# The first attention block reordered (keys hashed ahead of queries, the projection split on GpSimd, the second head turned inside unit zero's scores), and the token-buffer fills issued two units later

## Chip, cores and metric

The kernel runs on 1 core of one Trainium2 chip. The metric is the device time of one execution in microseconds (us), taken as the median of several runs. Before the change it is 513.87 us, the median of 3 runs from 513.18 to 513.99.

## What is computed

Three stages follow one another: attention masked by a hash of queries and keys (LSH), a mixture of experts with one expert per token, and a SoLU layer with a norm.

```python
q_bits = (np.einsum('bhsd,dk->bhsk', q, proj) > 0).astype(np.int64)
k_bits = (np.einsum('bhsd,dk->bhsk', k, proj) > 0).astype(np.int64)
q_bucket = np.sum(q_bits * 2 ** np.arange(n_bits), axis=-1)        # n_bits = 6, k the same
mask = q_bucket[:, :, :, None] == k_bucket[:, :, None, :]
scores = np.where(mask, scale * np.matmul(q, k.transpose(0, 1, 3, 2)), -1e9)
attn = np.exp(scores - np.max(scores, axis=-1, keepdims=True))
out = np.matmul(attn / (np.sum(attn, axis=-1, keepdims=True) + 1e-09), v)
...
h = np.maximum(x[mask] @ w1[e], 0.0); out[mask] = gate_w * eom * (h @ w2[e])   # per expert e
...
h = x @ w_in; solu = h * softmax(h); out = layer_norm(solu) * g_ln @ w_out
```

Shapes: q, k and v are [2, 8, 768, 64], proj is [64, 6], there are 8 experts and 1536 tokens of width 512.

## The kernel before

The 16 (batch, head) pairs are taken two heads at a time: eight blocks n = 0 to 7. A block has 12 units (two halves of the queries, three tiles of 128 queries, two heads), 96 units in all. `emit_s` (L592) writes a unit's scores with four TensorE matmuls: two multiply q (high and low halves in 16 bits) with k, two add the hash mask by multiplying the query's bit rows (tile `cm`, called "c") with the key's bit rows and low halves (tile "b"). `emit_max` (L602 to L606) takes the row maximum on VectorE, `emit_exp` (L617) the exponential on ScalarE, `steps_t` (L629, L631) transposes the result of the unit two before between the score matmuls, and `emit_pv` (L653) multiplies with v. A hand-written schedule orders everything: `at(i, f, slot)` hangs a background step on unit i, and `due` emits it there; each engine runs its instructions in the order in which the code emits them.

The hash bits need operands with the head dimension on the partitions. For blocks 1 to 7 GpSimd splits q and k (`split`, L367 to L382) and the DMA queue of SP turns them (`trans`, L394 to L406: q, then k, then the low halves b). Block 0 can't wait for that: `first` (L412 to L526) splits on VectorE, ScalarE and GpSimd and turns on TensorE (`pe`, L420), head 0 first. `q_hi`, `q_lo`, `k_hi` and `k_lo` are the splits; `bits_mm` (L542 to L548) multiplies with the split projection `pw`, and `bits_rows` (L554) compares the result with thresholds and writes the bit rows. `setup` (L215) splits the projection `pj` into `pw`: 15 small operations on VectorE and three copies on GpSimd. Head 1 of block 0 follows, turned before the first score matmul: its q and k transposes stand in front of unit 0's scores on TensorE.

Two more pieces matter. `setup_late`, hung on unit 2, loads the gate weights into `rg` and g_ln into `g1` with five small DMAs on SP's queue, behind a GpSimd memset of `rg`. `zero(e)`, hung on unit 8 + 4e, fills expert e's rows of the token buffer `xs` in DRAM with zeros from a tile that GpSimd clears once.

In `first`, the order in which head 0 is handled is this:

```python
q_t(0, pq); k_hi(0); k_t(0, pk)
act.copy(out=d["q", 0], in_=pq)
q_hi(1, True); k_lo(0); setup(); l_t(0, pl)
act.copy(out=d["k", 0], in_=pk)
...
bits_mm(0, "q", (0, 1), mq)
bits_mm(0, "k", (0, 1), mk)
```

Of the kernel before, what the change touches and what calls it, by code (L numbers as in the profile page):

```python
# [21 lines left out]
def kernel(  # L22
# [15 lines left out]
    nc = tc.nc  # L38
# [175 lines left out]
    def setup():  # L214

        NB2 = 2 * NBIT
        sc = early.tile([128, 512], I32, tag="db", name="db", bufs=2)[0:64]
        pi = sc[:, 0:NB2]
        pf = sc.bitcast(F32)[:, NB2:4 * NB2].rearrange("p (a b) -> p a b", a=3)
        p16 = sc.bitcast(F16)[:, 8 * NB2:13 * NB2].rearrange("p (a b) -> p a b", a=5)  # L220
        d = nc.vector
# [4 lines left out]
        d.tensor_copy(out=p16[:, 3], in_=pf[:, 0])  # L226
        d.tensor_scalar(out=pf[:, 1], in0=pi, scalar1=0.125, scalar2=None, op0=ALU.mult)
        d.tensor_tensor(out=p16[:, 4], in0=pf[:, 0], in1=p16[:, 3], op=ALU.subtract)
        d.tensor_tensor(out=pf[:, 2], in0=pf[:, 0], in1=pf[:, 1], op=ALU.subtract)
        d.tensor_copy(out=p16[:, 0], in_=pf[:, 1])  # L230
        d.tensor_copy(out=p16[:, 1], in_=pf[:, 2])
        o = slice(0, NB2)
        a, b = slice(0, 64), slice(64, 128)
        d.tensor_copy(out=pw[b, 1:3, o], in_=p16[:, 3:5])
        d.tensor_tensor(out=p16[:, 2], in0=pf[:, 2], in1=p16[:, 1], op=ALU.subtract)
        d.tensor_copy(out=pw[a, 8, o], in_=p16[:, 3])
        d.tensor_copy(out=pw[a, 7, o], in_=p16[:, 1])
        d.tensor_copy(out=pw[a, 0:3, o], in_=p16[:, 0:3])
        d.tensor_copy(out=pw[b, 7, o], in_=p16[:, 2])
# [20 lines left out]
    def setup_late():  # L260
        ie = const.tile([128, E], I32, name="ie")
        it = const.tile([128, B, NS], I32, name="it")
        g = nc.gpsimd
        g.memset(rg, 0.0)
# [6 lines left out]
        nc.sync.dma_start(out=g1, in_=g_ln.rearrange("(f p) -> p f", p=128))  # L271
        g.iota(ie, pattern=[[1, E]], base=0, channel_multiplier=0)
# [39 lines left out]
    def attention(es):  # L312
# [96 lines left out]
        def first():  # L409
# [21 lines left out]
            def q_hi(h, on_act):  # L431
                if on_act:
                    act.activation(out=tq[:, h, :, h], in_=q_[:, h], func=AF.Copy, scale=QK_S)
                else:
                    dve.tensor_scalar(out=tq[:, h, :, h], in0=q_[:, h], scalar1=QK_S, scalar2=None, op0=ALU.mult)

            def q_lo(h):
                dve.scalar_tensor_tensor(out=tq[:, h, :, 1 - h], in0=q_[:, h], scalar=QK_S, in1=tq[:, h, :, h],
                                         op0=ALU.mult, op1=ALU.subtract)
# [27 lines left out]
            def lo_pool(o, i, hi):  # L467
                nc.gpsimd.tensor_scalar(out=i, in0=i, scalar1=QK_S, scalar2=1.0, op0=ALU.mult, op1=ALU.mult)
                nc.gpsimd.tensor_tensor(out=o, in0=i, in1=hi, op=ALU.subtract)

# [4 lines left out]
            nc.gpsimd.memset(cm.bitcast(F32)[96:128, :, 0], 0.0)  # L475
            nc.gpsimd.memset(cm.bitcast(F32)[32:64, :, 1], 0.0)
            q_hi(0, False)
            q_lo(0)
# [12 lines left out]
            mq, mk = t32(ps_m, "m"), ps_s.tile([128, 2, 512], F32, tag="s", name="s")[:, 0]  # L491
# [6 lines left out]
            lo_pool(tq[:, 1, :, 0], q_[:, 1], tq[:, 1, :, 1])  # L498
            k_hi(1)
            lo_pool(tl[:, :, 1], k_[:, 1], tk[:, 1, :, 0])  # L500
            begin(1)
            pq1, pk1 = t16(ps_v, "v"), t16(ps_t, "t0")
            q_t(1, pq1)
            k_t(1, pk1)
            act.copy(out=d["q", 1], in_=pq1)
            act.copy(out=d["k", 1], in_=pk1)
            nc.gpsimd.tensor_copy(out=d["c", 1][row(1)], in_=d["q", 1][row(1)])
            mid = {}

            def later1():  # L510
                pl1 = t16(ps_v, "v")
                l_t(1, pl1)
                act.copy(out=d["b", 1][row(1)], in_=pl1[row(1)])
                bits_rows(0, "q", 1, mq)

            def later2():
                mid["q"], mk1 = t32(ps_m, "m"), t32(ps_v, "v")
                bits_mm(0, "q", (2, 3), mid["q"])
                bits_mm(0, "k", (2, 3), mk1)
                bits_rows(0, "q", 2, mid["q"])  # L520
                bits_rows(0, "k", 2, mk1)
                bits_rows(0, "k", 3, mk1)

            at(0, later1, slot=0)
            at(1, later2, slot=1)
            at(3, lambda: bits_rows(0, "q", 3, mid["q"]))  # L526
# [4 lines left out]
        def bits_mm(n, which, groups, m):  # L531

            d = op[n]
            for i in range(3):
                for g in groups:
# [5 lines left out]
                    if which == "q":  # L541
                        nc.tensor.matmul(o, pw[:, 3 * h + i], flat(d["q", h])[:, cs], tile_position=(0, 32 * g), **k_)  # L542
                    elif i < 2:
                        nc.tensor.matmul(o, pw[:, 7 * i], flat(d["k", h])[:, cs], tile_position=(0, 32 * g), **k_)
                    elif n == 0:
                        nc.tensor.matmul(o, pw[r, 8 + h], flat(d["b", h])[r, cs], tile_position=(64 * h, 32 * g), **k_)
                    else:
                        nc.tensor.matmul(o, pw[:, 8 + h], flat(d["b", h])[:, cs], tile_position=(0, 32 * g), **k_)  # L548

# [459 lines left out]
        for e in range(E):  # L1009
            at(8 + 4 * e, zero, e)  # L1010
# [22 lines left out]
    with tc.manual_schedule():  # L1033
        with ExitStack() as es:
# [14 lines left out]
            for i in range(NU):  # L1049
                a_("emit_s")(i, a_("steps_t")(i - 2) if 2 <= i else iter(()))  # L1050
# [457 lines left out]
```

## Time and profile before

| what | value |
|---|---|
| median of 3 runs | 513.87 us |
| profiled execution, its own time | 513.23 us |
| its span, first to last instruction | 511.5 us |
| TensorE busy | 496.9 us (97% of the span) |
| VectorE busy | 388.2 us (76%) |
| ScalarE busy | 320.9 us (63%) |
| GpSimd busy | 281.9 us (55%) |
| granted TensorE clock, mean | 0.999 |

Busy times count instructions between their recorded start and end. PE is TensorE's matmul side, PEld its weight loads, DVE is VectorE, ACT ScalarE, POOL GpSimd, SPq the DMA queue of SyncE. Attention takes the span up to about 235 us, the experts run to about 375 us, the last layer to the end.

### The profile page before, as it was taken

Reading aid. Unit: us, or ns where it says so; the run is one execution under the profiler, and the core shown is the slowest. Engines: PE = TensorE matmul, PEld = TensorE weight load, DVE = VectorE, ACT = ScalarE, POOL = GpSimd, SP = SyncE. Lnnn points to the kernel's source line nnn. Section 1 sums busy time; section 2 is a strip of 40 time slices with the busy share of each in tenths; the row PEclk is TensorE's granted clock in tenths of the full one; section 3 lists DMA queues with packets and bytes.
Section 4 is the critical chain, followed back from the end, with each engine's and each line's share of the span. In section 5 each row is a group of like instructions: output and inputs, shape, how many; then the busy total and the mean of one; then the engine's idle time right before and its main releaser. Section 6 shows DMA issues by size and latency. Waiting matters only on the chain. (4 is left out here: it accounts for less than half of the span.)

```text
span 511.5 us, 12503 instructions
## 1 busy us (share of the span) xinstructions
PE 496.9 (97%) x4716; PEld 385.1 (75%) x4716; DVE 388.2 (76%) x922; ACT 320.9 (63%) x601; POOL 281.9 (55%) x438
## 2 busy tenths in 40 slices
PE   7899999999999999999999999999999999999994
PEld 5678787888888887887999999999984444444443
DVE  7787888888889888877779799979935987656610
ACT  6778787887887788886256566556623445534421
POOL 6999897869879898644366587322012113221131
PEclk9999999999999999999999999999999999999999
DMA  7398969772946675500499999998800246442281
GB/s 263 57 214 185 245 162 232 195 204 78 187 142 108 187 202 121 161 1 22 157 305 278 318 309 271 268 324 277 279 12 0 42 82 97 108 106 62 62 145 41
DMA packets 107182, 83.21 MB, mean 163 GB/s; under 512 B 80624, under 2 KB 89456, under 8 KB 107120
## 3 DMA queue, kind: packets, MB, share of 16 engines
q1 hardware_dynamic: 104816, 76.09, 59.1%
q0 software_dynamic: 2304, 6.31, 3.2%
q8 instruction: 37, 0.61, 0.5%
q14 instruction: 25, 0.20, 0.1%
HBM read 51.43 MB, written 9.97 MB: 120 GB/s over the span
## 5 line engine op out<-in xcount | busy, mean ns | idle before, releaser
L629 PE MATMUL t<-ident,p 128*128 128x128 f32 x576 | 126.1, 275 | 0.6
L617 ACT ACTIVATE p<-s,mx 128x768 f32<-128x768 f32 x96 | 95.8, 998 | 36.4 <-DVE mx L606 22.5
L602 DVE TENSOR_REDUCE mx<-s 128x1 f32<-128x768 f32 x96 | 91.5, 953 | 28.4 <-PE s L592 22.4
L631 ACT COPY pt<-t 128x384 f32<-128x384 f32 x192 | 85.6, 480 | 7.4 <-PE t L629 6.2
L629 PEld LDWEIGHTS t<-ident,p 128*128 128x128 f32 x576 | 77.8, 141 | 15.6 <-ACT pt L631 9.0
L653 PE MATMUL v<-pt,v 128*64 128x128 f32 x1128 | 72.0, 277 | 0.0
L653 PEld LDWEIGHTS v<-pt,v 128*64 128x64 f32 x1128 | 60.6, 137 | 7.7 <-issue 6.8
L1446 PE MATMUL o<-wo,zT 128*128 128x512 f16 (+1 forms) x312 | 63.7, 363 | 0.1
L1246 PE MATMUL a<-hh,wb 128*128 128x224 f16 (+5 forms) x256 | 63.4, 251 | 0.1
L131 POOL TENSOR_SCALAR dm<-dm 128x512 f32<-128x512 f32 x16 | 33.0, 2061 | 55.5 <-ACT dm L126 55.3
L1374 PE MATMUL h<-wi,yT 128*128 128x512 f16 x288 | 63.5, 379 | 0.0
L1247 PE MATMUL a<-hh,wb 128*128 128x224 f16 (+5 forms) x256 | 63.4, 251 | 0.0
L1248 PE MATMUL a<-hh,wb 128*128 128x224 f16 (+5 forms) x256 | 63.4, 251 | 0.0
L592 PE MATMUL s<-k,q 128*128 128x384 f16 x192 | 59.0, 329 | 1.2 <-ACT p L617 1.2
L592 PE MATMUL s<-b,cm 128*128 128x384 f16 x192 | 57.2, 326 | 0.9 <-DVE b L554 0.9
L1219 PE MATMUL a<-xw,wa 128*128 128x224 f16 (+5 forms) x224 | 55.1, 249 | 0.0
L1218 PE MATMUL a<-xw,wa 128*128 128x224 f16 (+5 forms) x224 | 55.1, 249 | 0.0
L1217 PE MATMUL a<-xw,wa 128*128 128x224 f16 (+5 forms) x224 | 55.1, 249 | 0.0
L1446 PEld LDWEIGHTS <-zT 128*128 128x128 f16 x312 | 30.5, 98 | 32.2 <-issue 0.4
L1374 PEld LDWEIGHTS <-yT 128*128 128x128 f16 x288 | 28.2, 98 | 33.7
L1452 POOL DMA_INDIRECT out_dram<-o,tok x12 | 12.6, 1048 | 53.3 <-issue 42.4
L168 ACT ACTIVATE wb<-raw 128x1024 f16<-128x1024 f32 x24 | 25.3, 1055 | 22.1 <-DMA raw<-in_moe_w_dram 22.0
(275 smaller groups left out, 1017.7 us busy)
## 6 DMA issues: line engine op xcount, KB each, us to landing
raw<-in_moe_w_dram SPq DMA_DIRECT2D x64, 512.0 KB, 6.1
raww<-in_moe_w_in_dram SPq DMA_DIRECT2D x8, 512.0 KB, 5.1
raww<-in_moe_w_out_dram SPq DMA_DIRECT2D x8, 512.0 KB, 6.4
xs<-raw SPq DMA_DIRECT2D x8, 448.0 KB, 4.4
v<-in_v_dram SPq DMA_DIRECT2D x8, 384.0 KB, 6.7
q<-in_q_dram SPq DMA_DIRECT2D x6, 384.0 KB, 4.3
k<-in_k_dram SPq DMA_DIRECT2D x6, 384.0 KB, 6.5
cm<-q SPq DMA_DIRECT2D x14, 96.0 KB, 2.1
```

Source lines behind the costliest of these rows:

```text
L592: nc.tensor.matmul(t[:, c, 0:SB], d[x, h][:, s], flat(d[y, h])[:, c * SB:(c + 1) * SB], start=first, stop=not first)
L602: nc.vector.tensor_reduce(out=mx[:, 0:1], in_=t[:, :, 0:SB], op=ALU.max, axis=AX.XY)
L617: nc.scalar.activation(out=p, in_=s_t.pop(i)[:, :, 0:SB], func=AF.Exp, scale=mx[:, 1:2], bias=mx[:, 2:3], accum_out=sums[j][:, qt, h:h + 1])
L629: nc.tensor.transpose(t[:, g * 128:(g + 1) * 128], p[:, c, g * 128:(g + 1) * 128], ident)
L631: nc.scalar.copy(out=pt[i][:, 3 * c:3 * c + 3], in_=t[:, 0:SB].rearrange("p (g c) -> p g c", g=3))
L653: nc.tensor.matmul(o[64 * h:64 * h + 64], vt[:, h, c], ph[h][:, c], start=(c == 0), stop=(c == NS - 1), tile_position=(0, 64 * h))
L1217: nc.tensor.matmul(ps[:, i, 0:n], w[:, 0, kk, fs], xw[:, 0, kk], start=(kk == 0), stop=False)
L1246: nc.tensor.matmul(ps, w[:, 0, f, ds], hh[:, 0, f], start=(f == 0), stop=False)
L1247: nc.tensor.matmul(ps, w[:, 0, f, ds], hh[:, 1, f], start=False, stop=False)
L1248: nc.tensor.matmul(ps, w[:, 1, f, ds], hh[:, 0, f], start=False, stop=(f == KF - 1))
L1374: nc.tensor.matmul(ps[:, c], yT[:, a, kk, ts], w_i[:, w, kk, c * 512:(c + 1) * 512], start=(kk == 0 and a == 0 and w == 0), stop=(kk == KD ...
L1446: nc.tensor.matmul(ps, zT[:, KF * a + f], w_o[:, w, f, cs], start=(f == 0 and a == 0 and w == 0), stop=(f == KF - 1 and a == 1))
```

## The change

Four parts. (1) `pj` is loaded from ScalarE's DMA queue before anything else there, not from SP's between the second q and the second k. (2) `setup` is cut into four pieces; GpSimd does the nine steps that lead to the rounded projection and one copy into `pw`, VectorE two steps and four copies, and GpSimd's other three copies come after head 1's split. (3) In `first`, q of head 0 is split by VectorE and ScalarE in halves, k is copied out and hashed before q, both halves of the key bits are compared in one operation (`bits_k2`, at one tile position in two banks), head 1's low half of k moves from GpSimd to VectorE, and head 1's q and k are turned between unit 0's q-k and mask matmuls. The query bits of units 6 onward (`bits_rows` with groups 1 and 3) move to units 3 and 4. (4) The five gate and g_ln loads move from unit 2 to unit 0, their memset to the start; two memsets of `cm`, used by block 1, move from the start to unit 1; the fills of the token buffer move from unit 8 + 4e to unit 10 + 4e.

```diff
@@ setup
-        d.tensor_copy(out=pf[:, 0, 0:NBIT], in_=pj)
-        d.tensor_scalar(out=pf[:, 0, NBIT:], in0=pj, scalar1=-1.0, scalar2=None, op0=ALU.mult)
-        d.tensor_scalar(out=pi, in0=pf[:, 0], scalar1=8.0, scalar2=None, op0=ALU.mult)
...
-        nc.gpsimd.tensor_copy(out=pw[b, 9, o], in_=p16[:, 3])
-        nc.gpsimd.tensor_copy(out=pw[b, 3:6, o], in_=p16[:, 0:3])
-        nc.gpsimd.tensor_copy(out=pw[a, 4:6, o], in_=p16[:, 3:5])
+        def gpsimd():
+            g.tensor_copy(out=pf[:, 0, 0:NBIT], in_=pj)
+            g.tensor_scalar(out=pf[:, 0, NBIT:], in0=pj, scalar1=-1.0, scalar2=1.0, op0=ALU.mult, op1=ALU.mult)
+            g.tensor_scalar(out=pi, in0=pf[:, 0], scalar1=8.0, scalar2=1.0, op0=ALU.mult, op1=ALU.mult)
+            g.tensor_scalar(out=pf[:, 1], in0=pi, scalar1=0.125, scalar2=1.0, op0=ALU.mult, op1=ALU.mult)
+            g.tensor_tensor(out=pf[:, 2], in0=pf[:, 0], in1=pf[:, 1], op=ALU.subtract)
+            g.tensor_copy(out=p16[:, 0], in_=pf[:, 1])
+            g.tensor_copy(out=p16[:, 1], in_=pf[:, 2])
+            g.tensor_tensor(out=p16[:, 2], in0=pf[:, 2], in1=p16[:, 1], op=ALU.subtract)
+            g.tensor_copy(out=pw[a, 0:3, o], in_=p16[:, 0:3])
...
+        def vector_late():
+            d.tensor_copy(out=pw[b, 1:3, o], in_=p16[:, 3:5])
+            d.tensor_copy(out=pw[a, 8, o], in_=p16[:, 3])
+            d.tensor_copy(out=pw[a, 7, o], in_=p16[:, 1])
+            d.tensor_copy(out=pw[b, 7, o], in_=p16[:, 2])
@@ first
-            q_hi(0, False)
-            q_lo(0)
+            pool, pool_late, vec, vec_late = setup()
+            q_hi(0, False, half[0])
+            q_hi(0, True, half[1])
+            for a in half:
+                q_lo(0, a)
+            pool()
+            vec()
             pq, pk, pl = t16(ps_t, "t0"), t16(ps_t, "t1"), t16(ps_v, "v")
             q_t(0, pq)
             k_hi(0)
             k_t(0, pk)
+            act.copy(out=d["k", 0], in_=pk)
+            k_lo(0)
+            vec_late()
+            l_t(0, pl)
             act.copy(out=d["q", 0], in_=pq)
-            q_hi(1, True)
-            k_lo(0)
-            setup()
-            l_t(0, pl)
-            act.copy(out=d["k", 0], in_=pk)
+            dve.tensor_copy(out=d["b", 0][row(0)], in_=pl[row(0)])
             dve.tensor_copy(out=d["c", 0][row(0)], in_=d["q", 0][row(0)])
-            dve.tensor_copy(out=d["b", 0][row(0)], in_=pl[row(0)])
...
+            bits_k2(0, 0, mk)
             bits_mm(0, "q", (0, 1), mq)
-            bits_mm(0, "k", (0, 1), mk)
+            r = slice(64, 96)
+            nc.vector.tensor_scalar(out=flat(d["b", 0])[r].rearrange("p (b x) -> p b x", b=2), in0=mk[0:32, :, 0:SB],
+                                    scalar1=thr[r, 1:2], scalar2=-MASK, op0=ALU.is_le, op1=ALU.mult)
             bits_rows(0, "q", 0, mq)
-            bits_rows(0, "k", 0, mk)
-            bits_rows(0, "k", 1, mk)
...
+            def second():
+                yield
+                k_t(1, pk1)
+                act.copy(out=d["k", 1], in_=pk1)
+                q_t(1, pq1)
+                act.copy(out=d["q", 1], in_=pq1)
+                yield
...
-            at(3, lambda: bits_rows(0, "q", 3, mid["q"]))
+            at(3, lambda: bits_rows(0, "q", 1, mq))
+            at(4, lambda: bits_rows(0, "q", 3, mq))
+            return second()
@@ bits_k2 (new)
+            for i in range(3):
+                for c in range(2):
+                    cs = slice(c * SB, (c + 1) * SB)
+                    o = m[0:32, c, 0:SB]
...
+                        nc.tensor.matmul(o, pw[:, 7 * i], flat(op[n]["k", h])[:, cs], tile_position=(0, 0), **k_)
@@ the rest
-            at(8 + 4 * e, zero, e)
+            at(10 + 4 * e, zero, e)
+        nc.scalar.dma_start(out=pj, in_=proj)
-                if h == 1 and nm == "q":
-                    nc.sync.dma_start(out=pj, in_=proj)
-            A["first"]()
+            nc.gpsimd.memset(rg, 0.0)
+            second = A["first"]()
             A["load"](1)
+            A["at"](0, gate_load)
             A["at"](2, setup_late)
-                a_("emit_s")(i, a_("steps_t")(i - 2) if 2 <= i else iter(()))
+                a_("emit_s")(i, a_("steps_t")(i - 2) if 2 <= i else iter(()) if i else second)
```

`gate_load` is the part of `setup_late` that issued the five DMAs.

How the instructions move, first on TensorE, from the hash of head 0 to unit 0's mask matmuls (`tp` is a transpose in PSUM, `tb` and `s` hold hash sums, `s` also the scores, `qs` and `ks` are split q and k). Before:

```order
L542 MATMUL tb<-q_197,pw 32x384
...
L544 MATMUL s<-k_198,pw 32x384
...
L546 MATMUL s<-b_199,pw 32x384
...
L420 MATMUL tp<-ident_72,qs 128x128
...
L420 MATMUL tp<-ident_72,ks 128x128
...
L592 MATMUL s<-k_198,q_197 128x384
...
L592 MATMUL s<-b_199,cm 128x384
```

and now:

```order
L582 MATMUL s<-k_199,pw 32x384
...
L584 MATMUL s<-b_200,pw 32x384
...
L565 MATMUL tb<-q_198,pw 32x384
...
L628 MATMUL s<-k_199,q_198 128x384
...
L430 MATMUL tp<-ident_72,ks 128x128
...
L430 MATMUL tp<-ident_72,qs 128x128
...
L628 MATMUL s<-b_200,cm 128x384
```

The keys' hash now stands ahead of the queries', and head 1's transposes stand between unit 0's q-k and mask matmuls, k ahead of q.

On ScalarE, from its first instruction to head 1's copies. Before:

```order
L1027 ACT_TABLE_LOAD
L1027 ACTIVATE warm<-warm 128x1
L442 ACTIVATE ks<-k 128x768
L483 COPY q_197<-tp 128x768
L433 ACTIVATE qs<-q 128x6x64
L488 COPY k_198<-tp 128x768
L442 ACTIVATE ks<-k 128x768
L505 COPY q_274<-tp 128x768
L506 COPY k_275<-tp 128x768
```

and now:

```order
L1056 DMA pj<-in_proj_dram 64x6
L1062 ACT_TABLE_LOAD
L1062 ACTIVATE warm<-warm 128x1
L445 ACTIVATE qs<-q 128x3x64
L454 ACTIVATE ks<-k 128x768
L496 COPY k_199<-tp 128x768
L500 COPY q_198<-tp 128x768
L512 CAST qs<-q 128x6x64
L454 ACTIVATE ks<-k 128x768
L524 COPY k_272<-tp 128x768
L526 COPY q_271<-tp 128x768
```

The copy of k comes before that of q, and head 1's q split no longer stands between the two.

On SP's queue, from the last weight load of the start to block 1's transposes. Before:

```order
L182 DMA raw<-in_moe_w_dram 128x1024
L394 DMA_TRANSPOSE q_371<-qs 128x6x128
L394 DMA_TRANSPOSE q_373<-qs 128x6x128
L400 DMA cm<-q_371 64x768
L400 DMA cm<-q_373 64x768
L269 DMA rg<-in_moe_w_gate_dram 64x4x8
L269 DMA rg<-in_moe_w_output_gate_dram 64x4x8
L269 DMA rg<-in_moe_w_gate_dram 64x4x8
L269 DMA rg<-in_moe_w_output_gate_dram 64x4x8
L271 DMA g_93<-in_moe_g_ln_dram 128x8x1
L394 DMA_TRANSPOSE k_467<-ks 128x6x128
```

and now:

```order
L182 DMA raw<-in_moe_w_dram 128x1024
L274 DMA rg<-in_moe_w_gate_dram 64x4x8
L274 DMA rg<-in_moe_w_output_gate_dram 64x4x8
L274 DMA rg<-in_moe_w_gate_dram 64x4x8
L274 DMA rg<-in_moe_w_output_gate_dram 64x4x8
L276 DMA g_93<-in_moe_g_ln_dram 128x8x1
L404 DMA_TRANSPOSE q_377<-qs 128x6x128
L404 DMA_TRANSPOSE q_379<-qs 128x6x128
L410 DMA cm<-q_377 64x768
L410 DMA cm<-q_379 64x768
L404 DMA_TRANSPOSE k_467<-ks 128x6x128
```

The five small loads no longer stand between block 1's q and k transposes.

## Rows read from the trace of the kernel before

**Rows 1.** Stretches: from:to, length, busy (count) of PE, PEld, DVE, ACT, POOL, clock, DMA.

```profile
4.52:9.84 5.32, 3.70 (x45) 2.63 (x45) 5.04 (x22) 3.15 (x6) 2.97 (x7) 1.00 0.98 305
...
12.00:18.00 6.00, 3.94 (x31) 2.62 (x25) 5.31 (x12) 4.13 (x9) 5.75 (x10) 1.00 0.36 77
18.00:20.00 2.00, 1.93 (x11) 1.09 (x10) 1.18 (x3) 2.00 (x6) 2.00 (x5) 1.00 0.74 145
...
32.00:230.00 198.00, 197.72 (x2163) 161.69 (x2163) 164.96 (x409) 159.48 (x343) 162.61 (x252) 1.00 0.66 165
...
250.00:502.00 252.00, 251.72 (x2068) 185.94 (x2066) 184.15 (x364) 126.64 (x188) 81.30 (x84) 1.00 0.65 172
```

**Rows 2.** Timeline, first block: start us, us, engine, line, operation [idle before <-releaser].

```profile
0.73 1.28 ACT L1027 ACT_TABLE_LOAD   x1 [0.73 <-PEq L1492]
...
3.18 0.69 DVE L435 TENSOR_SCALAR qs<-q 128x384 f16<-128x384 f32 x1 [0.72 <-DMA q<-in_q_dram]
3.71 0.84 ACT L442 ACTIVATE ks<-k 128x768 f16<-128x768 f32 x1 [1.48 <-DMA k<-in_k_dram]
4.98 0.50 PE L420 MATMUL tp<-ident,ks 128*128 128x128 f16 x6
5.88 0.53 ACT L433 ACTIVATE qs<-q 128x384 f16<-128x384 f32 x1
6.30 0.79 ACT L488 COPY k<-tp 128x768 f16<-128x768 f16 x1
...
7.45 0.50 PE L544 MATMUL s<-k,pw 128*32 128x384 f16 x4
7.87 0.91 POOL L469 TENSOR_TENSOR qs<-q,qs 128x384 f16<-128x384 f32 x1
7.90 0.61 DVE L554 TENSOR_SCALAR cm<-tb,thr 32x384 f16<-32x384 f32 x1
7.92 0.34 PE L546 MATMUL s<-b,pw 64*32 64x384 f16 x2
8.43 1.24 DVE L554 TENSOR_SCALAR b<-s,thr 32x384 f16<-32x384 f32 x2
9.52 0.49 PE L592 MATMUL s<-k,q 128*128 128x384 f16 x2
9.84 0.49 PE L592 MATMUL s<-b,cm 128*128 128x384 f16 x2
```

**Rows 3.** Timeline of TensorE at block 1's key bits: hash, then unit 9's scores.

```profile
30.54 0.51 PE L544 MATMUL m<-k,pw 128*32 128x384 f16 x8
...
31.68 0.34 PE L548 MATMUL m<-b,pw 128*32 128x384 f16 x2 [0.26 <-DMA b<-kl]
31.95 0.34 PE L592 MATMUL s<-k,q 128*128 128x384 f16 x1
```

**Rows 4.** Timeline of TensorE at the same place of block 2.

```profile
59.26 0.51 PE L544 MATMUL m<-k,pw 128*32 128x384 f16 x8
...
59.86 0.34 PE L592 MATMUL s<-k,q 128*128 128x384 f16 x1
```

**Rows 5.** Timeline of SP's DMA queue, the gate loads and block 1's transposes.

```profile
20.59 0.68 SPq L269 DMA_DIRECT2D rg<-in_moe_w_gate_dram  x1
...
23.96 2.60 SPq L394 DMA_TRANSPOSE k<-ks  x2
26.61 3.54 SPq L406 DMA_TRANSPOSE b<-kl  x2
```

**Rows 6.** Landing of `pj` (view of that tile).

```profile
DMA to landing us min/median/max: 3.0/3.0/3.0
```

**Rows 7.** Timeline of two small GpSimd operations in a row.

```profile
21.84 0.20 POOL L280 TENSOR_SCALAR iota_s<-iota 128x8 f32<-128x8 f32 x1
22.11 0.20 POOL L281 TENSOR_SCALAR ord<-iota 128x8 f32<-128x8 f32 x1
```

**Rows 8.** The page's costliest groups: line, operation, count, busy us, mean ns.

```profile
L131 POOL TENSOR_SCALAR dm<-dm 128x512 f32<-128x512 f32 x16 | 33.0, 2061 | 55.5 <-ACT dm L126 55.3
```

More of the change, by code (lines that the diff above doesn't have):

```diff
@@ L229, in setup @@
-        d.tensor_tensor(out=pf[:, 2], in0=pf[:, 0], in1=pf[:, 1], op=ALU.subtract)
-        d.tensor_copy(out=p16[:, 0], in_=pf[:, 1])
-        d.tensor_copy(out=p16[:, 1], in_=pf[:, 2])
+        d, g = nc.vector, nc.gpsimd
         o = slice(0, NB2)
         a, b = slice(0, 64), slice(64, 128)
[L234 to L237, printed above, removed]
@@ new lines, in gpsimd_late, with vector @@
+        def gpsimd_late():
+            g.tensor_copy(out=pw[b, 3:6, o], in_=p16[:, 0:3])
+            g.tensor_copy(out=pw[a, 4:6, o], in_=p16[:, 3:5])
+            g.tensor_copy(out=pw[b, 9, o], in_=p16[:, 3])
+        def vector():
+            d.tensor_copy(out=p16[:, 3], in_=pf[:, 0])
+            d.tensor_tensor(out=p16[:, 4], in0=pf[:, 0], in1=p16[:, 3], op=ALU.subtract)
+        def vector_late():
[3 more added lines that the diff above has]
+            d.tensor_copy(out=pw[b, 7, o], in_=p16[:, 2])
@@ L244, in setup_first @@
+        return gpsimd, gpsimd_late, vector, vector_late
     def setup_first():
@@ L258, in setup_first, with gate_load @@
         d.scalar_tensor_tensor(out=thr[:, 0:1], in0=fi[:, 1:2], scalar=TINY, in1=fi[:, 2:3], op0=ALU.add, op1=ALU.add)
[L260 to L264, printed above, removed]
+    def gate_load():
         for h in range(2):
@@ L271, in setup_late @@
         nc.sync.dma_start(out=g1, in_=g_ln.rearrange("(f p) -> p f", p=128))
+    def setup_late():
+        ie = const.tile([128, E], I32, name="ie")
+        it = const.tile([128, B, NS], I32, name="it")
+        g = nc.gpsimd
         g.iota(ie, pattern=[[1, E]], base=0, channel_multiplier=0)
@@ L429, in begin, with q_hi, q_lo @@
                 nc.gpsimd.memset(d["b", h].bitcast(F32)[96 - 64 * h:128 - 64 * h], 0.0)
-            def q_hi(h, on_act):
+            half = slice(0, NS // 2), slice(NS // 2, NS)
+            def q_hi(h, on_act, a=slice(0, NS)):
                 if on_act:
-                    act.activation(out=tq[:, h, :, h], in_=q_[:, h], func=AF.Copy, scale=QK_S)
+                    act.activation(out=tq[:, h, a, h], in_=q_[:, h, a], func=AF.Copy, scale=QK_S)
                 else:
-                    dve.tensor_scalar(out=tq[:, h, :, h], in0=q_[:, h], scalar1=QK_S, scalar2=None, op0=ALU.mult)
-            def q_lo(h):
-                dve.scalar_tensor_tensor(out=tq[:, h, :, 1 - h], in0=q_[:, h], scalar=QK_S, in1=tq[:, h, :, h],
+                    dve.tensor_scalar(out=tq[:, h, a, h], in0=q_[:, h, a], scalar1=QK_S, scalar2=None, op0=ALU.mult)
+            def q_lo(h, a):
+                dve.scalar_tensor_tensor(out=tq[:, h, a, 1 - h], in0=q_[:, h, a], scalar=QK_S, in1=tq[:, h, a, h],
                                          op0=ALU.mult, op1=ALU.subtract)
@@ L494, in first @@
             bits_rows(0, "q", 0, mq)
-            bits_rows(0, "k", 0, mk)
-            bits_rows(0, "k", 1, mk)
-            lo_pool(tq[:, 1, :, 0], q_[:, 1], tq[:, 1, :, 1])
+            nc.gpsimd.tensor_scalar(out=q_[:, 1], in0=q_[:, 1], scalar1=QK_S, scalar2=1.0, op0=ALU.mult, op1=ALU.mult)
+            act.copy(out=tq[:, 1, :, 1], in_=q_[:, 1])
+            nc.gpsimd.tensor_tensor(out=tq[:, 1, :, 0], in0=q_[:, 1], in1=tq[:, 1, :, 1], op=ALU.subtract)
             k_hi(1)
-            lo_pool(tl[:, :, 1], k_[:, 1], tk[:, 1, :, 0])
+            k_lo(1)
@@ L501, in first @@
             begin(1)
[L502 to L508, printed above, removed]
+            pool_late()
+            nc.gpsimd.memset(fill[32:64, 0, 1], 0.0)
+            pk1, pq1 = t16(ps_t, "t0"), t16(ps_v, "v")
+            def second():
[5 more added lines that the diff above has]
+                yield
@@ L510, in later1 @@
             def later1():
-                pl1 = t16(ps_v, "v")
+                pl1 = t16(ps_t, "t1")
                 l_t(1, pl1)
                 act.copy(out=d["b", 1][row(1)], in_=pl1[row(1)])
-                bits_rows(0, "q", 1, mq)
+                nc.gpsimd.tensor_copy(out=d["c", 1][row(1)], in_=d["q", 1][row(1)])
             def later2():
-                mid["q"], mk1 = t32(ps_m, "m"), t32(ps_v, "v")
-                bits_mm(0, "q", (2, 3), mid["q"])
+                bits_mm(0, "q", (2, 3), mq)
@@ L548, in bits_mm, with bits_k2 @@
                         nc.tensor.matmul(o, pw[:, 8 + h], flat(d["b", h])[:, cs], tile_position=(0, 32 * g), **k_)
+        def bits_k2(n, h, m):
+            r = slice(64 * h, 64 * h + 64)
+            for i in range(3):
+                for c in range(2):
+                    cs = slice(c * SB, (c + 1) * SB)
+                    o = m[0:32, c, 0:SB]
+                    k_ = dict(start=(i == 0), stop=(i == 2))
+                    if i < 2:
+                        nc.tensor.matmul(o, pw[:, 7 * i], flat(op[n]["k", h])[:, cs], tile_position=(0, 0), **k_)
+                    else:
+                        nc.tensor.matmul(o, pw[r, 8 + h], flat(op[n]["b", h])[r, cs], tile_position=(64 * h, 0), **k_)
         def bits_rows(n, which, g, m):
```

20 lines of the change are left out of this document (7 added, 13 removed).

## The prediction

> **What bounds the kernel now.** The busy time by stretches comes first [rows 1]. From 32 to 230 us TensorE is busy 197.72 of 198.00 us, from 250 to 502 us 251.72 of 252.00. No other engine comes near: VectorE has 164.96 and 184.15 us there. So between attention's first units and the end there is nothing to save but TensorE's own work, of which the change removes none: it has the same matmuls in another order. What can move the time is the start, where TensorE waits: it idles 1.62 us from 4.52 to 9.84 us and 2.06 us from 12 to 18 us [rows 1]. A start that comes earlier moves everything behind it, since the rest runs end to end; it is not lost in a later wait unless one exists that doesn't move along.
>
> The timeline of the first block [rows 2] is read next, for the moment at which unit 0's scores are complete. The mask matmuls of unit 0 start at 9.84 us. Two chains end there almost together: VectorE's comparisons, of which the last ends at 9.67 us (8.43 + 1.24), and TensorE's order, in which head 1's q transposes wait for GpSimd's subtraction until 8.78 us (7.87 + 0.91), and the scores stand behind them. After unit 0 the order on VectorE (maximum, maximum, comparisons, maximum) repeats what it was, so that a gain at 9.84 us is carried to 18 us.
>
> Then the timeline of TensorE at block 1's key bits [rows 3] against block 2's [rows 4]. In block 2 the next scores start 0.60 us after the first key-hash matmul (59.26 to 59.86); in block 1 it is 1.41 us (30.54 to 31.95), with a wait for the DMA that brings b. The recorded idle time is only 0.26 us, since a matmul's record spans its whole passage; the start-to-start distance gives the loss, 0.81 us. That b is late has its reason on SP's queue [rows 5]: five small loads stand between block 1's q and k transposes, from 20.59 to 23.96 us.
>
> **The change part by part.** *First block.* k's split on ScalarE starts when k lands, at 3.71 us, and ends at 4.55. q's split gets two engines for its first step; VectorE's 0.69 us for the whole is at least 0.35 for half, so q's transposes can start between 0 and 0.5 us earlier. I take 0.2. k's transposes can't start before 4.55, nor before those of q; they ended at 5.48 (4.98 + 0.50) and I put them at 5.28. Then ScalarE copies k (0.79) to 6.1 us, q to 6.8, splits head 1's q (0.53) and k (0.84); it starts an instruction about 0.1 us before the recorded end of the one before (5.88 + 0.53 against 6.30), so these end near 7.2 and 7.95 us.
>
> The VectorE chain: the key hash starts at 6.13. Before, its six matmuls took 0.81 us (7.45 to 8.26), four of them two by two side by side, and the last two likewise. Now both halves stand at one tile position, one behind the other. Two 384-column matmuls in a row on the full array are 0.32 us from start to start of the next two (9.52 to 9.84), 0.16 each; six rounds in place of three add at least 0.32 beyond what overlapped rounds show, up to 0.48. I take 7.3 us for its end. One comparison of 768 in place of two of 384 lies between 0.61 and 1.24 us; I take 1.0, since the operation's fixed part is saved once. The query comparison (0.61) follows and ends near 9.0 us.
>
> The TensorE chain: k's transposes of head 1 start at 8.0, q's wait for GpSimd's subtraction, which follows the split at 7.2 and takes 0.91, to 8.15; both are out by 8.9 us. So the mask matmuls of unit 0 start near 9.0 us, against 9.84: **0.84 us earlier**. Bounds: 0 (one of the chains takes all that the other saves) and 1.2 (q's transposes 0.5 earlier, the comparison at 0.8).
>
> The Trainium skill, TensorEngine Tiling (Array Packing), section Tiling Modes, says that tiles at different positions work independently and in parallel; by that rule `bits_k2` gives away a concurrency that the kernel had. The trace agrees, since four 384-column matmuls take 0.50 us there and two in a row on the full array 0.49 [rows 2]; without the loss the sum would be about 0.3 us better.
>
> *The projection on GpSimd.* `pj` lands 3.0 us after its issue [rows 6]. From ScalarE's queue the issue can stand where the table load starts now, at 0.73 us [rows 2], so it lands near 3.75; the table load ends about 0.6 us later than at 2.0, still ahead of 3.18, where q lands, and costs nothing. Nine dependent GpSimd steps at 0.27 us from start to start [rows 7] end near 6.2, level with k's copy at 6.1. I cost it at nothing; the cover is the copy of k and it is thin: any step slower by 0.1 us is 0.1 us later on the path.
>
> The Trainium skill, GPSIMD Engine Reference, section Engine selection, speaks against it: it gives two-input elementwise work about half VectorE's speed there, and one-input work about the same. By it the two subtractions in the chain would add an estimated 0.2 to 0.3 us, and the sum below would be 512.5 in place of 512.2. No row of before shows GpSimd with a two-input operation that small.
>
> *Gate loads.* Before, SP's k transposes waited for five issues, 3.37 us (20.59 to 23.96). Moved ahead, they stand in SP's queue where it idled until block 1's q was split, so k and b come about 3.4 us earlier, or 4.2 with the start's 0.84. TensorE needs b 0.84 us earlier. That is ample, and the loss of **0.81 us** goes. Bounds: all of it, or nothing, and then 0.84 more is waited for (a rival below). What is late next there is the last weight of the hash itself, so the distance becomes that of block 2.
>
> *Comparisons moved.* The query comparison of 0.61 us that leaves unit 0's front comes back between units 3 and 4. VectorE is busy 1.18 of 2.00 us from 18 to 20 [rows 1]; that idle time hides it, and if it didn't, 0.61 us would be lost. *Token-buffer fills.* They pass on SP's queue from a place beside q's transposes to one between q's and k's. The cover is that later blocks' b is there in time [rows 4]; were one block's b as late as block 1's, it would cost 0.81 us. The two moved memsets are on GpSimd behind block 1's split, ahead of nothing that TensorE waits for.
>
> **The sum.** 0.84 + 0.81 = 1.65 us. The profiled execution took 513.23 us (a span of 511.5 and 1.7 around it): 511.6. The median of the runs is 0.64 above that execution, so the forecast for the median is **512.2 us**, 0.32% less. A measurement of this kernel can tell about 0.2%, 1.0 us, from no change.
>
> **The rivals.** *One term alone* (chance 0.22). If the first block gains nothing because the GpSimd chain or the comparisons take the place of what they replace, 0.81 remains and the time is 513.1. If b lands as late as before, TensorE waits at the same moment as now: 0.84 is given back, and the time is 513.9. For the first speaks how level three chains stand at 6.1 and 9.0 us; against the second speak the 3.4 us that leave SP's queue.
>
> *Slower through GpSimd's chain* (0.07). Two of the nine steps write or read 32-bit integers. No row shows GpSimd do that; the farthest row is the 2.06 us of L131 [rows 8], on 512 elements where these have 12. At that price each, two steps add 3.6 us: the chain ends at 9.8, and unit 0 starts 2.8 us later than now; less 0.81, the time is near 515.8. It decides once the chain ends later than 7.75 us (6.1 + 0.84 + 0.81), which is 0.44 us a step. The 0.20 us of small steps [rows 7] speak against it.
>
> *More than forecast* (0.06). The upper bounds together, 1.2 + 0.81, give 511.9, and a little less if later DMA waits shrink too.
>
> **How the numbers follow.** The forecast has 0.65. Its own spread, 0.4 us to either side, stays past 1.0 us of gain nearly always; with the case of more this is faster by over 0.2% with 0.67. The case of one term alone and the edge of the forecast are within 0.2%: 0.26. Slower is the GpSimd case: 0.07. The range takes in both bounds of the first block and most of the one-term case: 511.7 to 513.5.
>
> **What would show it.** Unit 0's mask matmuls at 9.0 us (8.6 to 9.8) instead of 9.84. At block 1's key bits, 0.60 us from the first hash matmul to the next scores and no wait for the DMA of b. GpSimd's last of nine steps near 6.2 us. TensorE's idle time from 32 to 230 and 250 to 502 us unchanged. The forecast is wrong if TensorE's scores of unit 9 don't start about 1.65 us earlier than 31.95, or if they do and a later stretch idles more.

## The result and the profile after

The changed kernel takes **518.0 us** (median of 6 runs, 516.34 to 519.37) against 513.8 for the kernel before beside it (6 runs, 513.18 to 514.6): a ratio of 1.0079, 95% interval 1.0062 to 1.0096. It is slower by 0.8%; 0.3% faster was forecast, and the range ended at 513.5. The profiled execution took 518.73 us with a span of 517.0 (513.23 and 511.5 before).

Both profiles are compared by the start of each unit, TensorE's first k,q score matmul of it, read from the timelines. A shift below is that start less the same unit's start before; minus is earlier.

| unit (its start before) | 1 (10.77) | 8 (27.67) | 9 (31.95) | 13 (40.97) | 15 (45.28) | 24 (65.98) | 25 (68.84) | 26 (70.16) | 95 (231.11) |
|---|---|---|---|---|---|---|---|---|---|
| shift after | -0.06 | -0.06 | -0.86 | -0.90 | -0.46 | -0.49 | +4.47 | +5.27 | +5.48 |

Three things are in this row. The first block gives 0.06 us where 0.84 was forecast. Between units 8 and 9 the gate loads give 0.80 where 0.81 was forecast. And between the starts of units 24 and 26, the first of block 2, 5.76 us are lost, where nothing was forecast.

The stretches of the changed kernel (columns as in [rows 1]):

```profile
12.00:18.00 6.00, 3.93 (x29) 2.56 (x25) 5.28 (x13) 4.27 (x9) 5.70 (x10) 1.00 0.44 63
18.00:20.00 2.00, 1.90 (x12) 1.12 (x12) 1.21 (x2) 2.00 (x6) 2.00 (x4) 1.00 0.67 132
32.00:230.00 198.00, 194.77 (x2096) 158.44 (x2095) 160.70 (x399) 155.23 (x332) 162.81 (x251) 0.98 0.65 158
250.00:502.00 252.00, 251.06 (x2081) 187.17 (x2080) 188.48 (x388) 127.08 (x189) 83.43 (x87) 1.00 0.65 175
```

Against [rows 1], TensorE idles 3.23 of 198 us from 32 to 230 where it idled 0.28, and the granted clock is 0.98 there. That stretch, which the prediction took for closed, holds the loss. TensorE's timeline shows the place:

```profile
62.22 1.53 PE L689 MATMUL v<-pt,v 128*64 128x128 f32 x24
...
65.49 0.32 PE L628 MATMUL s<-k,q 128*128 128x384 f16 x1
...
68.97 0.48 PE L628 MATMUL s<-b,cm 128*128 128x384 f16 x1 [2.77 <-DMA b<-raw]
...
70.55 2.83 PE L689 MATMUL v<-pt,v 128*64 128x128 f32 x24
...
75.43 0.33 PE L628 MATMUL s<-k,q 128*128 128x384 f16 x1
```

Unit 24's mask matmuls wait 2.77 us for the DMA that copies the key-bit rows into b. Behind the wait the 24 value matmuls take 2.83 us, against 1.53 at 62.22. The granted clock says why (TensorE alone; length, busy, clock, DMA share, GB/s):

```profile
68.00:69.00 1.00, 0.03 (x1) 0.58 0.54 144
69.00:70.00 1.00, 1.00 (x5) 0.50 1.01 256
74.00:75.00 1.00, 1.00 (x6) 0.51 0.56 91
75.00:76.00 1.00, 1.00 (x9) 1.00 0.38 83
```

TensorE stood idle, then ran at 1.2 GHz from 69 to 75 us, and at 2.4 again from 75. So the loss in this execution has two halves: 2.95 us of delay at unit 24's mask matmuls (from -0.50 to +2.45) and 2.8 more until unit 26.

By the clock, the second half is not in every run. A slow stretch like this one (68.16 to 74.98 us by the trace's clock record, at half clock) takes about 0.007 off a run's mean granted clock. Of the six timed runs, three have a mean of 0.992 to 0.995 and took 517.68 to 519.37 us; three have 0.996 to 0.998, as the runs of the kernel before have (0.996 to 0.999), and still took 516.34 to 518.33. So most of the loss is there also where the mean clock shows no such stretch.

Why are the rows late? SP's waits (waited for: us in total, times, longest), then its timeline:

```profile
SPq L320 <- POOL raw L317: 5.3, 1, 5.3
```

```profile
32.30 2.41 SPq L610 DMA_DIRECT2D b<-raw  x4
40.12 0.36 SPq L320 DMA_DIRECT2D xs<-raw  x1
...
49.91 0.58 SPq L320 DMA_DIRECT2D xs<-raw  x1
50.59 3.25 SPq L404 DMA_TRANSPOSE k<-ks  x2
53.93 3.56 SPq L416 DMA_TRANSPOSE b<-kl  x2
57.55 0.56 SPq L182 DMA_DIRECT2D raw<-in_moe_w_dram  x1
...
63.19 4.26 SPq L610 DMA_DIRECT2D b<-raw  x4
```

The first fill (`xs<-raw`) waits 5.3 us for GpSimd to clear the zero tile. `zero(0)` issues that memset itself, so moving the fill two units later moved the memset behind more of GpSimd's work. GpSimd's timeline has it in the changed kernel and before:

```profile
39.13 0.96 POOL L317 MEMSET raw<- 128x1024 f32 x1
```

```profile
32.76 0.94 POOL L307 MEMSET raw<- 128x1024 f32 x1
```

Everything behind the fill on SP's queue waits with it, and the DMA engines have nothing to do (the last three columns are clock, DMA share and GB/s):

```profile
36.00:38.00 2.00, 2.00 (x23) 1.00 0.01 4
38.00:40.00 2.00, 2.00 (x30) 1.00 0.03 8
...
64.00:66.00 2.00, 2.00 (x23) 1.00 1.03 383
```

What was held is then issued late: block 2's k transposes at 50.59 (48.39 before), the large loads from 57.55 (54.94 before). The b rows themselves are issued only 0.4 us later than before. SP's timeline and the stretch of the kernel before:

```profile
48.39 2.58 SPq L394 DMA_TRANSPOSE k<-ks  x2
...
54.94 0.43 SPq L182 DMA_DIRECT2D raw<-in_moe_w_dram  x1
...
62.78 3.67 SPq L574 DMA_DIRECT2D b<-raw  x4
```

```profile
64.00:66.00 2.00, 2.00 (x26) 1.00 0.34 109
```

But the DMA engines are still full of those loads: their share from 64 to 66 us is 1.03, where it was 0.34. The rows' time from issue to landing (view of tile b, 56 to 70 us):

```profile
DMA to landing us min/median/max: 2.4/3.3/5.7
```

The trace holds the landing of three of the four copies here: the first took 5.7 us, the third 3.3, the fourth 2.4. Before, the same view reads 1.8, 2.0 and 2.3, but from the third and fourth copy alone (2.3 and 1.8). The first copy, which unit 24's first mask matmul reads, has no landing in that trace; it was there by 66.52, 3.7 us after its issue at the latest, since the mask matmuls start then without a wait. Seven profiles of the experiments hold it, at 3.6 to 4.8 us. The changed kernel's, issued at 63.19, arrives at 68.9; the matmul starts at 68.97.

### The profile page after: what moved, and what is told of

It reads as the page before. It is cut to its first block, busy times and chain, and to the rows that moved or that the text cites. A ratio compares the mean times of both kernels' runs of the same rounds, so it can differ in the third digit from the quotient of the medians.

```text
span 517.0 us, 12505 instructions
## 1 busy us (share of the span) xinstructions
PE 501.1 (97%) x4716; PEld 387.7 (75%) x4716; DVE 387.9 (75%) x914; ACT 321.8 (62%) x602; POOL 282.7 (55%) x447
## 5 line engine op out<-in xcount | busy, mean ns | idle before, releaser
L689 PE MATMUL v<-pt,v 128*64 128x128 f32 x1128 | 73.3, 280 | 0.0
L689 PEld LDWEIGHTS v<-pt,v 128*64 128x64 f32 x1128 | 61.7, 139 | 7.9 <-issue 6.8
```

Source lines behind the costliest of these rows:

```text
L689: nc.tensor.matmul(o[64 * h:64 * h + 64], vt[:, h, c], ph[h][:, c], start=(c == 0), stop=(c == NS - 1), tile_position=(0, 64 * h))
```

## The experiments

Each kernel below was timed in 3 or 5 rounds against the kernel before, in three sessions; its medians there were 513.95, 513.76 and 513.64. The shifts are read from each kernel's one profile.

| kernel | median us | ratio, 95% interval | unit 8 | unit 9 | unit 15 | unit 26 | unit 95 |
|---|---|---|---|---|---|---|---|
| changed | 518.0 | 1.0079 [1.0062, 1.0096] | -0.06 | -0.86 | -0.46 | +5.27 | +5.48 |
| fills_back | 515.24 | 1.0017 [0.9996, 1.0037] | +0.44 | -0.36 | +0.46 | +0.84 | +1.04 |
| fills_only | 517.79 | 1.0060 [1.0037, 1.0083] | -0.17 | -0.30 | -0.33 | +3.95 | +4.02 |
| clear_early | 514.52 | 0.9993 [0.9973, 1.0013] | -0.06 | -0.86 | -0.36 | -0.47 | -0.25 |
| bridge | 517.79 | 1.0064 [1.0045, 1.0084] | +0.26 | -0.54 | -0.15 | +2.34 | +2.64 |
| gates_only | 513.11 | 0.9982 [0.9966, 0.9998] | +0.03 | -0.77 | -0.68 | -0.80 | -0.88 |
| first_only | 516.66 | 1.0048 [1.0027, 1.0069] | -0.07 | +1.65 | +1.63 | +1.74 | +2.04 |
| warm_new | 513.35 | 0.9998 [0.9980, 1.0015] | -0.36 | -1.17 | -0.62 | -0.28 | +0.01 |
| warm_old | 513.66 | 1.0000 [0.9983, 1.0017] | -0.12 | -0.41 | -0.44 | -0.45 | -0.37 |
| best_new | 513.37 | 0.9994 [0.9980, 1.0009] | -0.89 | -1.70 | -1.15 | -1.27 | -1.02 |
| gates_warm | 512.96 | 0.9989 [0.9978, 0.9999] | -0.09 | -0.90 | -0.69 | -0.81 | -0.56 |
| gates_again | 512.87 | 0.9981 [0.9964, 0.9998] | +0.33 | -0.47 | -0.24 | -0.35 | -0.38 |

From unit 95 to the end the profiled executions add between -0.1 and +2.3 us on the kernel before, with no order that the edits explain; the kernel before alone ran from 513.0 to 517.4 us. So a place is judged by its shift, and a kernel by its ratio.

**fills_back**, the changed kernel with the fills at the old units:

```
-            at(10 + 4 * e, zero, e)
+            at(8 + 4 * e, zero, e)
```

> The changed kernel with the token-buffer fills back on units 8 + 4e; all else as changed. Theory A, the fills' new place on SP's queue makes block 2's key bit rows late at unit 24 (the 2.77 us wait for DMA b<-raw) and the clock falls behind that wait: no wait at unit 24, the clock stays up, and the 0.77 us that unit 23 was ahead stays to the end: about 513.0 us. Theory B, the rows are late because of the other parts (gate loads moved, block 1's transposes earlier): the wait stays and the time is near 518.

Against the kernel before, 0.2% is left of the 0.8%, and the long stall at unit 24 is gone (0.23 us of waiting for b are left there), but it is not faster than the kernel before. Two things stand against it. Its first block ended 0.5 us later than the changed kernel's (below). And the wait has moved to block 1 (TensorE, then SP):

```profile
39.11 0.32 PE L628 MATMUL s<-b,cm 128*128 128x384 f16 x1 [0.69 <-DMA b<-raw]
```

```profile
35.30 0.35 SPq L320 DMA_DIRECT2D xs<-raw  x1
35.75 1.39 SPq L610 DMA_DIRECT2D b<-raw  x2
```

The fill, still waiting for its clear, stands ahead of block 1's b rows, so unit 12 waits for them: from -0.37 to +0.46 in one unit. The clear itself, at its old unit, runs at 34.32 us in place of 32.76: besides the late first block, the two memsets of `cm` that the change moved stand ahead of it on GpSimd. The fills' two later units do serve a purpose: in the changed kernel block 1's b rows are issued from 32.30 on, ahead of the fill. They only pass the delay to block 2.

**fills_only**, the kernel before with the fills two units later (the same line, the other way).

> The kernel before with nothing changed but the fills on units 10 + 4e. Theory A: the wait appears at unit 24, shorter by the 0.8 us by which TensorE gets there later, and the clock falls behind it: 517 to 518.5 us. Theory B: no change, 513.9 us. If the wait is there but too short to bring the clock down: about 516.

That one line makes the kernel before slower by 0.6%. Its profile shows the same wait for b at unit 24, and unit 26 is 4.2 us later against unit 24 (from -0.29 to +3.95):

```profile
68.89 0.48 PE L592 MATMUL s<-b,cm 128*128 128x384 f16 x1 [2.49 <-DMA b<-raw]
```

The fills' move is the cause of the loss, without the rest of the change. Its runs differ in clock as the changed kernel's do: five with a mean of 0.994 or 0.995 have a median of 518.26 us, five with 0.996 to 0.999 one of 516.93. An estimate from these two groups gives the fall of the clock 1.3 us, less than half of the loss.

**clear_early**, the changed kernel with the fills where they are, but the memset of the zero tile issued on its own at unit 8:

```
+    def zero_tile():
+        z = raw.tile([128, 1024], F32, tag="raw", name="raw")
+        nc.gpsimd.memset(z, 0.0)
+        zt[0] = z
...
     def zero(e):
-        if e == 0:
-            z = raw.tile([128, 1024], F32, tag="raw", name="raw")
-            nc.gpsimd.memset(z, 0.0)
-            zt[0] = z
...
+        at(8, zero_tile)
```

> The changed kernel, fills on units 10 + 4e, but the tile of zeros is taken and cleared by GpSimd on unit 8, as before, so that SP's queue doesn't wait for the clearing (5.3 us of waiting, to 40.12 us). Theory A1, the waiting SP queue does it: everything behind the first fill is earlier by several us, no wait at unit 24, about 513.0 us. Theory A2, the fills' place among the transposes and bit rows does it: the wait stays, 516 to 518 us.

The memset runs at 33.84 us, the first fill goes out at 34.81, and the DMA engines, idle before, are full in the same stretch:

```profile
36.00:38.00 2.00, 2.00 (x23) 1.00 1.04 265
38.00:40.00 2.00, 2.00 (x30) 1.00 0.92 250
```

The wait and the fall of the clock at unit 24 are gone (unit 26 at -0.47). The fills are at the changed units all the same, and the second stands ahead of block 2's k transposes as in the changed kernel. So it is SP's 5.3 us behind the clear that makes the long wait, not the fills' new place in the queue. The median is within 0.2% of the kernel before: the gain that remains is no longer one that can be measured.

**bridge**, the changed kernel with 16 score matmuls of unit 24 repeated ahead of it, which adds work and keeps TensorE busy while the rows arrive:

```
+            for _ in range(16 if i == 24 else 0):
+                nc.tensor.matmul(t[:, 0, 0:SB], d["q", h][:, s], flat(d["k", h])[:, 0:SB], start=True, stop=True)
```

> The changed kernel with 16 more matmuls of 384 columns ahead of unit 24's scores, into the bank that those then overwrite; they compute nothing that is used. At 0.16 us each they fill 2.6 us of the 2.77 us that TensorE waits. Theory C, about half of the 5.76 us lost between units 23 and 27 is the clock at half speed from 68.2 to 75.1 us, after the engine had idled: no fall of the clock, and the time is 2.5 to 3 us shorter, about 515.2 us. Rival, all of it is waiting for DMA: about 518, or more.

The 16 matmuls fill 65.72 to 68.32 us, the rows are there behind them, and the granted clock stays at 1.00:

```profile
65.72 2.76 PE L627 MATMUL s<-k,q 128*128 128x384 f16 x16
...
69.72 1.53 PE L691 MATMUL v<-pt,v 128*64 128x128 f32 x24
```

From unit 23 to unit 26 this kernel loses 2.6 us (from -0.25 to +2.34), against 5.76 in the changed kernel: between these two profiles, the half that lay behind the wait was the clock. The time does not follow. The median is 517.79 us, where 515.2 was expected, and nine of the ten runs have a mean clock of 0.996 or more, so the filler kept the clock up and the kernel is no faster than the changed one for it. In the profile, 0.3 us of the rest are lost in the first block and 1.6 in the last stages; where the medians lose it is open.

**gates_only**, the kernel before with the gate loads moved ahead as in the change (their function cut out of `setup_late`), and nothing else:

```
             A["first"]()
+            nc.gpsimd.memset(rg, 0.0)
             A["load"](1)
+            A["at"](0, gate_load)
```

> The kernel before with only the gate loads moved ahead (and the memset of their tile with them); the first block and the fills as before. The gate term: at block 1's key bits the distance from the first hash matmul to the next scores shrinks from 1.41 to about 0.60 us, so unit 9 stands about 0.81 us earlier. Theory A (SP's queue sets the rows of the blocks' bits): the first fill is issued ahead of block 1's b rows, as in fills_back, where TensorE waited 0.69 us for them at unit 12; so part or all of the 0.81 is lost again at unit 12, and from unit 13 on the kernel stands 0 to 0.4 us earlier: 513.5 to 514.0 us. Rival: the rows come in time, unit 13 keeps the 0.81, and the median is near 513.1.

The rival held: no wait comes back at units 12 or 24, and the shift is kept (-0.77 at unit 9, -0.88 at unit 95). TensorE at block 1's key bits, to lay beside [rows 3]:

```profile
30.57 0.51 PE L545 MATMUL m<-k,pw 128*32 128x384 f16 x8
30.91 0.34 PE L549 MATMUL m<-b,pw 128*32 128x384 f16 x4
31.18 0.34 PE L593 MATMUL s<-k,q 128*128 128x384 f16 x1
```

0.61 us from the first hash matmul to the next scores, and no wait. The clear of the zero tile runs at 32.75 us here, and block 1's b rows go out at 34.18, against 34.32 and 35.75 in fills_back, so unit 12 does not wait. This part alone is 0.2% faster than the kernel before. **gates_again** is the same kernel in another session:

> gates_only a second time, beside the two others, for a second median of the smallest edit that gained: 512.8 to 513.4 if its 0.65 us were the edit's own, 513.5 or more if they were the spread between sessions.

512.87, ratio 0.9981 after 0.9982: the gain repeats, though both intervals end just short of no change (0.9998).

**first_only**, the changed kernel with gate loads and fills in their old places, so that the first block alone is new:

```
     def setup_late():
...
+        g.memset(rg, 0.0)
+        gate_load()
...
-            at(10 + 4 * e, zero, e)
+            at(8 + 4 * e, zero, e)
...
-            nc.gpsimd.memset(rg, 0.0)
...
-            A["at"](0, gate_load)
```

> The changed kernel with the gate loads back in their old place and the fills at the old units, so that only the first block is new. Theory A: unit 0's mask matmuls start between 9.7 and 10.3 us as in the other runs of the new first block, since its transposes run at half clock; whatever is gained there is lost at block 1's key bits, where TensorE waits for b as long as before or longer, so unit 9 stands within 0.5 us of 31.95 and the time is within 1 us of the kernel before. Rival (the first block costs nothing, all loss is the fills): unit 9 is 0.3 us earlier or more and the median below 513.7.

Slower by 0.5%, and worse than either theory had it. Unit 9 is 1.65 us late: block 1's k transposes start at 25.22 us on SP's queue, 1.26 later than before, because the gate loads ahead of them start at 21.84 in place of 20.59. They wait for the memset of `rg` on GpSimd, and the two memsets of `cm` that the change put behind block 1's split (0.41 us each) now stand ahead of it. In the whole change the gate loads are gone from there, so this costs nothing; the parts of this change can't be judged one by one.

**warm_new**, clear_early with 30 warm-up matmuls on a tile of ones that VectorE writes first:

```
+        nc.vector.memset(ones16, 1.0)
...
-            for _ in range(24):
-                nc.tensor.matmul(w[:, 0:128], ident16, ident16, start=True, stop=True)
+            for _ in range(30):
+                nc.tensor.matmul(w[:, 0:128], ones16, ones16, start=True, stop=True)
```

> The kernel of clear_early with the warm-up matmuls on a tile of ones that VectorE writes first, so that they start near 1.0 us in place of 2.0 (30 in place of 24). Theory D (the first block's term was lost to the clock): the granted clock rises before the transposes of k, these take 0.50 us in place of 0.85, the key hash starts near 6.3 in place of 6.91, and unit 0's mask matmuls stand near 9.1 us in place of 9.77; unit 24 stands about 1.4 us earlier than in the kernel before, and the median is 0.6 us under clear_early's, near 513.6. Rival: the clock rises no earlier, or another chain ends at 9.77 anyway; then the mask matmuls stay between 9.7 and 10.1 and the median near 514.5.

The warm-up starts at 1.05 us, yet k's transposes still take 0.85 us: theory D is not shown by this run. Its mask matmuls start at 9.47, 0.30 earlier than in clear_early, because the first transposes start 0.30 earlier (4.23 in place of 4.53), behind a warm-up that leaves TensorE's queue sooner. At unit 24, which comes 0.74 us earlier than before, a wait for b is back (0.29 us of idle time, and the shift goes to -0.28), with the fills at the changed units; best_new below, with the fills at the old ones, has none. That points to a small cost of the fills' new place once TensorE comes this early, but best_new also clears the tile earlier, so it is not shown.

**warm_old**, the kernel before with the same edit, and **gates_warm**, gates_only with it:

> The kernel before with the same earlier warm-up. Theory D: in the old order the clock does not set the end of the first block (its mask matmuls stood at 9.84 us with the clock up at 4.80 and at 9.66 with the clock up at 7.49), so they stay between 9.5 and 9.9 us and the median within 0.5 us of the kernel before. Rival: they come 0.4 us earlier or more, and the gain of the new order with an early clock would then not be its own.

> The kernel before with the gate loads ahead and the earlier warm-up. The gate term: unit 9 stands 1.0 to 1.2 us earlier than in the kernel before and keeps it to unit 25; the median is 512.8 to 513.3. Rival: the wait comes back at unit 12 or 24 for a block's bit rows, and the median is near that of the kernel before.

Nearly as expected (the rise that the first text puts at 7.49 us stands at 7.43 in fills_only's record): unit 0's mask matmuls start at 9.72 and 9.75 us, the first median is that of the kernel before, and gates_warm stands 0.90 earlier at unit 9 (1.0 to 1.2 was expected) and keeps 0.81 up to unit 26.

**best_new**, warm_new with the fills at the old units and the memset at unit 4:

```
-            at(10 + 4 * e, zero, e)
+            at(8 + 4 * e, zero, e)
...
-        at(8, zero_tile)
+        at(4, zero_tile)
```

> The changed kernel with the earlier warm-up of warm_new, the fills back at the old units and the zero tile cleared on unit 4, so that SP has no fill to wait for. Theory A: neither block 1's nor block 2's bit rows are late, so no wait for b stands at units 12 and 24 (0.69 us in fills_back, 0.29 in warm_new); unit 9 stands about 1.4 us earlier than in the kernel before and unit 25 by 0.9 or more; the median is 512.5 to 513.2. Rival (VectorE's work near unit 13 and the later stages take it back whatever SP does): unit 25 stands 0.5 to 0.7 us earlier as in warm_new, and the median is 513.2 to 513.7.

This profile is the one that shows what the first block can do. Here k's six transposes take 0.50 us and everything follows (TensorE's timeline):

```profile
4.69 0.50 PE L431 MATMUL tp<-ident,ks 128*128 128x128 f16 x6
...
6.08 0.81 PE L583 MATMUL s<-k,pw 128*32 128x384 f16 x4 [0.32 <-ACT k L497]
...
8.94 0.50 PE L629 MATMUL s<-b,cm 128*128 128x384 f16 x2
```

Against the changed kernel's:

```profile
5.17 0.85 PE L430 MATMUL tp<-ident,ks 128*128 128x128 f16 x6
5.95 0.85 PE L430 MATMUL tp<-ident,kl 128*64 128x128 f16 x6
6.91 0.81 PE L582 MATMUL s<-k,pw 128*32 128x384 f16 x4
...
9.77 0.50 PE L628 MATMUL s<-b,cm 128*128 128x384 f16 x2
```

And fills_back's, whose instructions are the changed kernel's up to here:

```profile
6.91 1.31 PE L582 MATMUL s<-k,pw 128*32 128x384 f16 x4
8.15 0.49 PE L584 MATMUL s<-b,pw 64*32 64x384 f16 x2
...
10.27 0.34 PE L628 MATMUL s<-b,cm 128*128 128x384 f16 x1
```

In one order of work the same four hash matmuls take 0.81 or 1.31 us and the same six transposes 0.50 or 0.85, and unit 0 comes at 8.94, 9.77 or 10.27. The longer stand to the shorter as 1.6 and 1.7 to 1, near the value matmuls' 2.83 to 1.53 at the clock's two levels. The view of stretches reads 1.00 from the start in every run and can't tell them apart, since the trace's clock record, which no view prints, begins only when the clock is up. But the record's first entry fits in all thirteen profiles: it stands at 4.48, 4.73 and 4.80 us in the three whose transposes took 0.50 us, and at 5.95 to 7.96 in the ten others. The changed kernel's is at 6.71, ahead of its hash matmuls at 6.91; fills_back's is the last of all, 7.96. That the clock was at its lower level until then is inferred from this and from the durations; what sets the moment of the rise stays open. The old order hardly feels it: with k's transposes at 0.50 us its mask matmuls stood at 9.84 and 9.75 (before, gates_warm), and with 0.84 or 0.85 at 9.66 to 10.17 (fills_only, warm_old, both runs of the gate edit). No wait for b stands at units 12 or 24, as expected; but 0.58 us are lost between units 13 and 15. The shift at unit 25, -1.26, is the theory's and not the rival's; the median, 513.37, is the rival's. So the gain is there in this profile; in the medians it is too small to be measured.

## Why the prediction was wrong

**The step that failed** is the sentence on the fills: "The cover is that later blocks' b is there in time; were one block's b as late as block 1's, it would cost 0.81 us". It failed three times. The fill was seen as a transfer that changes its place on SP's queue, but its first one carries a GpSimd memset, which moved too, and SP stood 5.3 us behind it. The cover was read from [rows 4], which only show that nothing waited, not how much room there was; block 2's b rows were issued from 62.8 to 65.9 us before, and unit 24's first mask matmul stood at 66.52. And the price was taken from a wait of 0.81 us, where unit 24 waited 2.77 us and, in the profiled execution, the clock fell behind the wait and cost as much again.

**The gate loads** were right in mechanism and size: 0.80 us between units 8 and 9 in the changed kernel and in every kernel that has them ahead, against 0.81 worked out from [rows 3, 4]; the distance there is 0.61 us against the 0.60 forecast:

```profile
30.48 0.51 PE L567 MATMUL m<-k,pw 128*32 128x384 f16 x8
30.82 0.33 PE L571 MATMUL m<-b,pw 128*32 128x384 f16 x4
31.09 0.34 PE L628 MATMUL s<-k,q 128*128 128x384 f16 x1
```

**The first block's** 0.84 was mis-sized, 0.06 in the profile of the changed kernel. The step is "k's transposes ... I put them at 5.28": they ended at 6.02 (5.17 + 0.85), and the 0.74 us passed down the chain to the mask matmuls at 9.77 in place of 9.0. The order on paper was right: best_new has them at 8.94, and unit 9 there is 1.70 us earlier, where 1.65 was forecast. What was wrong was to take durations of 0.50 us from one profile, which turned out to be among the quick ones: of the twelve other profiles here, ten have 0.84 or 0.85 us for these transposes. The new order puts TensorE's transposes and the hash at the head of the longest chain, so it feels this, while the old one had other chains as long.

**Smaller steps held.** One comparison of 768 took 1.01 us (1.0 taken), the hash matmuls at one position 0.81 in place of 0.50. GpSimd's nine steps ended at 5.84 us (6.2 forecast), ahead of the start of k's copy at 6.06, so the rival through that chain did not occur; its two-input steps took 0.22 and 0.20 us, where its one-input ones took 0.18 to 0.21 (one took 0.56) and VectorE had taken 0.20 and 0.16 for the same two subtractions before. The Trainium skill's rule (GPSIMD Engine Reference, section Engine selection) of half VectorE's speed for such work does not show at 12 elements a partition. The moved comparison cost nothing: the shift is -0.06 from unit 3 to unit 8.

**"It is not lost in a later wait"** was too strong. Between units 13 and 15 the changed kernel gives back 0.44 us and best_new 0.58, while gates_only, which comes there almost as early, gives back 0.13 and has it again at unit 23, where the changed kernel stands at -0.50. ScalarE waits there for VectorE's maximum (1.39 us at 38.80 in the changed kernel, 1.00 at 39.27 before). That VectorE's load in this stretch sets the pace is a reading; no run tried it.

The forecast gave 0.07 to slower, and that to a mechanism that did not occur; the one that did stood in a half sentence without a chance of its own.

## What to carry to other kernels

When a transfer is moved, move everything that it waits for in the mind too: what fills its source, on which engine, and what stands behind it in the queue that issues it. "Nothing waits there" is not a margin; read how long the data lay ready before it was used, for each block, and price a wait of a few microseconds on TensorE together with the slow stretch that may follow it. Where a chain is built from durations at the very start of a kernel, look at more than one execution before taking them.

## What was not expected of the hardware

Behind a wait of 2.77 us the granted clock fell in the changed kernel's profile, and it stayed at 0.50 for about 6 us with TensorE busy from 69 us on; behind the 2.49 us in fills_only it was up again at 72.3 us by the trace's clock record. The wait of 0.69 us at unit 12 in fills_back left no slow stretch behind it. Of the timed runs of both kernels only half have a mean clock that tells of such a stretch. At the kernel's start the same transposes took 0.50 us in some executions and 0.85 in others, with the same warm-up ahead of them; a warm-up that began 0.8 us earlier did not settle it (0.85 in warm_new, 0.84 in warm_old, 0.50 in best_new and gates_warm).
